# Five z1 copy buffers gated by sent stores, two attention output buffers, output weights halved earlier, and the last division taken step by step

## The chip, the cores and the metric

The kernel runs on one core of a Trainium2 chip. The metric is the device time of one execution in microseconds (us); before the change it is 1816.94 us, the median of three runs from 1816.54 to 1818.18. The core has five engines with an instruction stream each: PE (matrix products), DVE (vectors), ACT (activations and copies), POOL (vectors too) and SP, which here issues nearly all transfers. Each engine takes its instructions in the program's order, and an instruction that waits for another engine or a transfer holds up those behind it.

## The reference

The input x has 2048 rows of 576. A layer norm is followed by two branches, and their product is added to x.

```python
xn = layernorm(x)
# attention: 32 heads of 18, window of 256 keys
q, k, v = split(xn @ wqkv)
s = softmax(where(in_window, q k^T / sqrt(18), -1e9)) @ v        # then heads joined
s = s @ wo                                                       # 576 x 576
# gated unit: 2304 channels on each side
z1, z2 = split(gelu(xn @ w_in))
g = w_sp @ layernorm(z2) + b_sp                                  # 2048 x 2048 over the rows
out = x + s * silu((z1 * g) @ w_out)
```

All of it is float32, and the kernel reaches that precision by splitting operands into a high and a low part and taking several products.

## The kernel before

The program is written out engine by engine, in one long sequence. Its stages follow each other on PE: the q, k and v projections; the z2 half of the gated unit's first product (L210) up to about 430 us; the attention, 430 to 857 us; the output product with `wo` (L1314) up to about 925 us; the product over the rows (L1589) up to about 1610 us; and the last product (L1681).

**The attention stage** works in 16 units: eight groups of four heads for the first half of the rows (units 0 to 7), then the same groups for the second half (units 8 to 15). For each unit PE makes score products for the row maxima (L642), whose maxima DVE takes (L646), and the scores themselves (L787). ACT turns a bank of scores into probabilities in a `pt` tile (L791, called the exponential below), POOL blanks what is outside the window (L800, L803), and PE multiplies by the values into the accumulator `ops` (L817), in two halves of 512 columns. ACT copies each finished half into the unit's buffer `ou` (L831). Between these, PE fills in products of the z1 half of the gated unit (L723). Those end in one of seven PSUM banks (named `ma`, `mb`, `s0` to `s2`, `t0`, `t1`), which the scores use as well; DVE (L731) or ACT (L734) copies a finished block into a `z1o` buffer, of which there are three, and SP stores it (issued through L598, `z_d<-z1o` in the profile).

**The division** by the softmax sums follows each unit as a chain of nine steps: SP moves the sums out of `ou` (L867, `den<-ou`), DVE takes the reciprocal (L871), SP writes it to memory (L875, `r_d<-den`) and reads it back spread over the partitions (L879, `rp<-r_d`, four transfers; there is one `rp` buffer), POOL multiplies `ou` by it in four instructions of 256 columns (L891, the divides), and SP stores the four heads (L901, `o_d<-ou`, four transfers). There are three `ou` buffers, so the first copy of unit u waits for the stores of unit u - 3.

**What sets the order** is a planner that runs while the program is written. It keeps a `clock`, advanced by estimated PE times, and estimated finishing times of the other engines, and emits whatever is due: a score, a maximum, a group of value products, or, if nothing else is ready, one step of a z1 block (`can_fill`). SP's transfers are jobs with a due time (`issue`, `send`, `tick`); `flush` sends one at once when something is about to need it. The division steps come due `DEN_NS`, `SUM_NS` and `DIVIDE_NS` after one another, and `step(u, k)` emits at once every step of unit u up to k that has not been emitted. `step(u - 3, ...)` stands ahead of the allocation of unit u's `ou` buffer, so that the stores which that buffer waits for stand in the program before the copy. Heads of the next units are loaded by SP (L554, `att<-st_d`) and count as there `HEAD_NS` after their transfers. All these times are the planner's own; on the chip an instruction waits for its semaphores.

**Output weights and the end.** `wo` is loaded in five slices (L1097 and the ones it calls) while the last unit runs and split into two parts by DVE (L1101, L1102). The attention output is read back by `wo_load` (L1069, L1071) and split by `wo_split` (ACT L1300, DVE L1301) for the output product. The last unit's chain is emitted as far as its `rp` loads in the attention stage; its two divides stand ahead of the output product and its stores in pass 4 of 16.

Of the kernel before, what the change touches and what calls it, by code (L numbers as in the profile page):

```python
# [46 lines left out]
DIVIDE_NS = (9000, 6500, 4800)  # L47
SP_NS = 520
MOVE_NS = 5500
HEAD_NS = 5500  # L50
# [7 lines left out]
PTB = 7  # L58

# [10 lines left out]
def kernel(  # L70
# [169 lines left out]
    with ExitStack() as early:  # L240
# [283 lines left out]
        with ExitStack() as ph:  # L524
# [63 lines left out]
            sp_jobs = []  # L588
# [5 lines left out]
            def send(job, at):  # L594
                nonlocal sp_free
                sp_jobs.remove(job)
                sp_free = at + SP_NS
                job[-1]()  # L598
# [53 lines left out]
            def max_split(u):  # L652

                mx = maxima.pop(u)
                ms = halved[:, 0:64].rearrange("p (a n b) -> p a n b", a=4, n=2)
                dve.tensor_copy(ms[:, :, 0], mx)
                dve.tensor_tensor(ms[:, :, 1], mx, f32(ms[:, :, 0]), ALU.subtract)
                return use("dve", 500)
# [50 lines left out]
            def z1_rows(r):  # L709

                for f in range(FH // P):
# [7 lines left out]
                    for b in range(2):  # L719
                        bank, ps = take()  # L720
                        bank_of[r] = bank
                        for n, (w, x_) in enumerate(moving_x(wh, wl, slice(b * 512, (b + 1) * 512), r)):
# [3 lines left out]
                            if n == STEPS - 1:  # L726
                                flush(("zo", outs[0] - 3))
                                zo = zw.tile([P, 512], F32, name="z1o", bufs=3)
                                bank_of[r] = None
                                if max(busy["dve"], clock + 200) + 620 < max(busy["act"], clock + 200) + 480:  # L730
                                    dve.tensor_copy(zo, ps)  # L731
                                    bank_free[bank] = use("dve", 600, 140) + 100
                                else:
                                    act.activation(zo, ps, AF.Copy)  # L734
                                    bank_free[bank] = use("act", 480, 120) + 100
                                issue(partial(sp.dma_start, z1_tokens[f * P:(f + 1) * P, b, :, r],
                                              zo.rearrange("p (a q) -> p a q", a=2)),
                                      1000, bank_free[bank] - clock + 1300, ("zo", outs[0]))
                                outs[0] += 1
# [66 lines left out]
            def pv(u, kb, qa, qz):  # L806
# [18 lines left out]
                if kb == 4 * c + 3:  # L825
                    if c % 2 == 0:
                        step(u - 3, len(STAGES))
                        ous[u] = (ap_.tile([P, HS], F32, name="ou", bufs=3) if u < NU - 1 else
                                  tail()[:, 0:HS])
                    ou = ous[u]  # L830
                    act.activation(ou[:, c % 2 * 512:c % 2 * 512 + 512], o_ps.pop(c), AF.Copy)  # L831
                    free_at = use("act", 500, 120)
                    ops_free[0] = free_at
                    for t in later:
                        t[0] = free_at
                    if c % 2 == 1:
                        finish(u, ou)
                        if u + 2 < NU:
                            load_v(u + 2)
# [9 lines left out]
            def finish(u, ou):  # L849
# [53 lines left out]
                if u == NU - 1:  # L903
                    chain[u] = [load_den, invert, keep_den, all_sums]
                    last.extend([lambda: [divide(a, 2) for a in range(2)], lambda: [store(i) for i in range(4)]])
# [175 lines left out]
            def wow(i, k):  # L1081
                m = 5 * i + k
                return slots[2 + m // 4][:, (HS if m > 7 else 0) + m % 4 * D:(HS if m > 7 else 0) + (m % 4 + 1) * D]
# [11 lines left out]
            def load_wo(k):  # L1095
                raw = wors[k % 3]
                sp.dma_start(raw, wo[:, k, :])  # L1097

                def halve():
                    hi, lo = wow(0, k), wow(1, k)  # L1100
                    dve.tensor_copy(hi, raw)  # L1101
                    dve.tensor_tensor(lo, raw, f32(hi), ALU.subtract)  # L1102
                    use("dve", 1300)
# [7 lines left out]
            with ExitStack() as heads:  # L1111
# [74 lines left out]
                def can_fill(r):  # L1186
                    return bank_of[r] is not None or free_bank() is not None
# [31 lines left out]
                while score_queue[0] or score_queue[1] or todo or filling:  # L1219
# [43 lines left out]
                    if u == NU - 1 and n % 4 == 0 and 3 <= n // 4 < 8:  # L1263
                        wo_splits.pop(0)()
                    if u == NU - 1 and n % 4 == 0 and n // 4 < 5:
                        if n == 0:
                            step(u - 3, len(STAGES))
                            wors = [tail()[:, HS:HS + D],
                                    ap_.tile([P, HS], F32, name="ou", bufs=3)[:, :D]]
                        if n == 8:  # L1270
                            wors.append(ap_.tile([P, 10, 89], F32, name="vg").rearrange("p a b -> p (a b)")[:, :D])
                        load_wo(n // 4)
                    if u == NU - 1 and n == 28:
# [8 lines left out]
        with ExitStack() as ph:  # L1282
# [4 lines left out]
            stores = [zp.tile([P, D], F32, name="so") for _ in range(2)]  # L1287
# [30 lines left out]
            divide, store = last  # L1318
# [3 lines left out]
            divide()  # L1322
            pump(4, 5)
            for n in range(NS):
                t, c = divmod(n, 2)
                po = wo_half(0, *first_halves[0]) if n == 0 else wo_half(c * (t > 0), *halves_of[t])
                if n == 4:
                    store()
                    oraws.append(wo_load(4))
                if n in (0, 4, 6, 8):  # L1330
                    oraws.append(wo_load(3 + n // 2))
# [10 lines left out]
                so = zp.tile([P, D], F32, name="so")  # L1342
# [506 lines left out]
```

## Time and profile before

| | before |
|---|---|
| median of three runs | 1816.94 us (1816.54 to 1818.18) |
| the profiled execution: its time, and the span of its instructions | 1820.35 us, 1818.6 us |
| mean granted PE clock | 0.995 |
| PE / DVE / ACT / POOL busy | 1792.4 / 1145.2 / 930.4 / 432.0 us |

The profile comes from one execution, whose time was 3.4 us above the median; the span is the time from its first to its last instruction. A row of the waits gives engine, tile and line, what was waited for, the total in us, the number of times and the longest. A row of the chain of waits gives start, duration and what the last-ending work was doing. A row of the windows gives start and end, length, then for PE, PE's weight loads, DVE, ACT and POOL the busy time with the number of instructions, the mean granted PE clock (1.00 is full), the busy share of the transfer engines and GB/s. A row of a timeline gives start, duration, engine, line, operation, output and inputs, shapes, and in brackets how long the engine had been idle before it and what ended that.

### The profile page before, as it was taken

What the parts mean: (1) busy time and instruction counts of PE and PEld (TensorE: products, weight loads), DVE (VectorE), ACT (ScalarE), POOL (GpSimd) and SP (SyncE); (2) the same over time, 40 slices, a digit from 0 to 9 for tenths busy, and PEclk for the clock granted to TensorE, in tenths of its full rate; (3) what the DMA queues carried; (4) which work ended last, traced back from release to release, by engine and by line L of the source; (5) the groups of instructions that cost most, each with busy time, mean ns of one, the idle gap of its engine ahead of it and who ended that gap; (6) DMA issues with size and microseconds to landing.
All of it is one profiled execution on the core that took longest, in us unless ns stands there. A gap on an engine that the chain in (4) does not pass through costs nothing.

```text
span 1818.6 us, 37725 instructions
## 1 busy us (share of the span) xinstructions
PE 1792.4 (99%) x14391; PEld 1586.1 (87%) x14391; DVE 1145.2 (63%) x2322; ACT 930.4 (51%) x1737; POOL 432.0 (24%) x507
## 2 busy tenths in 40 slices
PE   9999999998999999998999999999999999999998
PEld 8989999998888888786988888888888888899998
DVE  7320243366877767663257697778876567768876
ACT  6432222224566676666467665466454534544443
POOL 3332334334456655556000000113000000000000
PEclk9999999999999999999999999999999999999999
DMA  8895779878567778756877768789786556797554
GB/s 283 201 241 155 255 257 312 271 231 265 148 188 199 206 191 198 184 151 167 257 240 239 250 216 278 263 284 300 240 271 236 174 187 208 243 275 214 155 156 137
DMA packets 266916, 405.72 MB, mean 223 GB/s; under 512 B 52336, under 2 KB 180592, under 8 KB 266608
## 3 DMA queue, kind: packets, MB, share of 16 engines
q1 hardware_dynamic: 266736, 403.32, 72.5%
q8 instruction: 113, 1.85, 0.4%
q14 instruction: 67, 0.55, 0.1%
HBM read 285.35 MB, written 117.09 MB: 221 GB/s over the span
## 4 chain that ended last, share of the span: by engine, by line
PE 85%; DMA 5%; DVE 5%; SPq 2%; issue 1%; ACT 1%; POOL 1%; DVEq 0%; ACTq 0%; POOLq 0%
PE acc L1589 31%; PE mb L210 10%; PE ma L210 10%; PE c L1681 8%; PE s L723 6%; PE ops L817 4%; PE t L723 4%; PE wops L1314 3%; PE ma L723 1%; PE s L642 1%; PE mb L723 1%; DVE spl L120 1%; DMA wr<-t_d 1%; PE s L787 1%; PE ma L384 1%
## 5 line engine op out<-in xcount | busy, mean ns | idle before, releaser
L1589 PE MATMUL acc<-spl,zh 128*128 128x512 f32 x1008 | 392.3, 389 | 0.7 <-DVE spl L120 0.7
L1589 PE MATMUL acc<-sph,zl 128*128 128x512 f32 x1008 | 392.1, 389 | 0.0
L1589 PE MATMUL acc<-sph,zh 128*128 128x512 f32 x1008 | 392.1, 389 | 0.0
L120 DVE TENSOR_TENSOR spl<-spr,sph 128x1024 fp32r<-128x1024 f32 x168 | 212.1, 1263 | 35.0 <-ACT sph L119 34.0
L1589 PEld LDWEIGHTS acc<-spl,zh 128*128 128x128 f32 x1008 | 189.2, 188 | 40.6 <-DVE spl L120 1.3
L1589 PEld LDWEIGHTS acc<-sph,zl 128*128 128x128 f32 x1008 | 189.2, 188 | 39.4
L1589 PEld LDWEIGHTS acc<-sph,zh 128*128 128x128 f32 x1008 | 189.2, 188 | 39.0
L119 ACT ACTIVATE zh<-b 128x384 fp32r<-128x384 f32 x168 | 87.6, 521 | 235.3 <-PE acc L1589 232.7
L119 ACT ACTIVATE sph<-spr 128x1024 fp32r<-128x1024 f32 x168 | 176.0, 1048 | 6.9 <-DMA spr<-sc_d 4.4
L723 PE MATMUL s<-b,z1wh 64*128 64x512 f32 x576 | 176.8, 398 | 0.0
L120 DVE TENSOR_TENSOR zl<-b,zh 128x384 fp32r<-128x384 f32 x168 | 98.6, 587 | 121.2 <-ACT zh L119 121.2
L646 DVE CUSTOM_DVE_ANT_0 s<-s,band 128x384 f32<-128x384 f32 (+2 forms) x231 | 125.2, 563 | 38.0 <-PE s L642 24.6
L1681 PE MATMUL c<-b,o 128*128 128x288 f32 x1056 | 143.1, 295 | 0.2 <-DVE o L120 0.2
L1681 PEld LDWEIGHTS c<-b,o 128*128 128x128 f32 x1056 | 140.8, 188 | 0.5 <-DVE o L120 0.4
L723 PE MATMUL t<-b,z1wh 64*128 64x512 f32 x414 | 137.0, 398 | 0.0
L791 ACT ACTIVATE pt<-s 128x384 f32<-128x384 f32 (+2 forms) x262 | 113.9, 456 | 40.6 <-PE s L787 28.6
L1046 DVE BATCH_NORM_STATS2 st<-zt 128x6 f32<-128x384 f32 x96 | 49.3, 548 | 131.8 <-ACT zt L1045 131.5
L210 PE MATMUL mb<-z2w,b 64*128 64x384 f32 x648 | 117.8, 336 | 0.0
L210 PE MATMUL ma<-z2w,b 64*128 64x384 f32 x648 | 117.7, 336 | 0.0
L800 POOL TENSOR_SCALAR_AFFINE_SELECT pt<-pt 128x512 f32<-128x512 f32 x128 | 81.8, 640 | 149.7 <-ACT pt L791 148.9
L210 PEld LDWEIGHTS mb<-z2w,b 64*128 64x128 f32 x648 | 114.1, 185 | 0.0
L210 PEld LDWEIGHTS ma<-z2w,b 64*128 64x128 f32 x648 | 114.1, 185 | 0.0
(268 smaller groups left out, 4793.5 us busy)
## 6 DMA issues: line engine op xcount, KB each, us to landing
spr<-sc_d SPq DMA_DIRECT2D x96, 512.0 KB
spr<-in_w_sp_dram SPq DMA_DIRECT2D x72, 512.0 KB
zr<-z_d SPq DMA_DIRECT2D x144, 192.0 KB
z_d<-zt SPq DMA_DIRECT2D x48, 384.0 KB
z_d<-z1o SPq DMA_DIRECT2D x72, 256.0 KB
z1t<-z_d SPq DMA_DIRECT2D x72, 256.0 KB
y_d<-z1t SPq DMA_DIRECT2D x72, 256.0 KB
a<-in_w_sp_dram SPq DMA_DIRECT2D x64, 256.0 KB
```

The lines of the kernel that those rows point to most:

```text
L119: act.activation(hi, src, AF.Copy)
L120: dve.tensor_tensor(lo, src, f32(hi), ALU.subtract)
L210: pe.matmul(banks[h][:, :n], *both[h][i], start=i == 0, stop=i == STEPS - 1)
L646: dve.tensor_tensor_reduce(out=ps[:, :w], in0=ps[:, :w], in1=band[:, m0:384], scale=1.0, scalar=-3.0e38, op0=ALU.add, op1=ALU.max, accum_o ...
L723: pe.matmul(ps, w, x_, start=n == 0, stop=n == STEPS - 1)
L791: act.activation(pt[:, j, d0:d0 + n * P], ps[:, (qa - a) * P:(qa - a + n) * P], AF.Exp, scale=scale)
L800: pool.affine_select(out=pt[:, :, 0:P], in_=pt[:, :, 0:P], pattern=[[0, 4], [1, P]], compare_op=ALU.is_ge, fill=0.0, base=0, channel_multi ...
L817: pe.matmul(o_ps[c][32 * j:32 * j + 32, (qa - 4 * c) * P:(hi - 4 * c + 1) * P], vgs[u][:, kb - k0, j * VW:j * VW + 32], pt[:, j, (qa - kb) ...
L1046: dve.bn_stats(st2[:, s, pc, :], zv)
L1314: pe.matmul(po[:, i, :288], lt[:, cs], r[:, i * 288:(i + 1) * 288], start=n == 0, stop=n == len(pl) - 1)
L1589: pe.matmul(acc[j], z[:, ps], w[:, cs], start=s == i == 0 and n in OPENS, stop=s == 7 and i == 2, skip_group_check=True)
L1681: pe.matmul(banks[key][:, :288], y, w, start=begin and k == n == 0, stop=close and k == 8 and n == 2, skip_group_check=True)
```

## The change

The constants and code change in five ways.

- `z1o` has five buffers in place of three. A z1 block may now be begun only if the store that frees its buffer has been sent, by the planner's book (`sent`). The stores come due 500 after the copy and not 1300.
- `ou` has two buffers in place of three, so unit u's first copy waits for the stores of unit u - 2, and `step(u - 2, ...)` emits their steps ahead of it.
- The planner takes loaded heads as there after 8500 and not 5500, the first unit groups' divides as due after 6500 and not 9000, and the split of the maxima as 1100 and not 500.
- The `wo` slices are loaded in unit 14 (three, into a slot that is free by then) and unit 15 (two, one of them into an `ou` buffer after the stores of unit 13), and split at five places of units 14 and 15, by DVE or ACT.
- The last unit's chain is emitted only as far as its sums. Its reciprocal, the write, the `rp` loads, the divides and the stores stand ahead of pass 0 and behind passes 0, 1, 2 and 3 of the output product; the reads of later parts move to passes 0, 5, 6, 7 and 9, and the output copies get three buffers.

The numbers of PE's instructions of each kind stay the same. Line numbers of the changed file are two or more higher: L831 becomes L833, L891 L893, L901 L903, L731 L733.

```diff
-DIVIDE_NS = (9000, 6500, 4800)
+DIVIDE_NS = (6500, 6500, 4800)
...
-HEAD_NS = 5500
+HEAD_NS = 8500
...
+ZOB = 5
...
-            sp_jobs = []
+            sp_jobs, sent = [], set()
...
             def send(job, at):
                 nonlocal sp_free
                 sp_jobs.remove(job)
+                sent.add(job[3])
...
                 dve.tensor_tensor(ms[:, :, 1], mx, f32(ms[:, :, 0]), ALU.subtract)
-                return use("dve", 500)
+                return use("dve", 1100)
...
-                                flush(("zo", outs[0] - 3))
-                                zo = zw.tile([P, 512], F32, name="z1o", bufs=3)
+                                flush(("zo", outs[0] - ZOB))
+                                zo = zw.tile([P, 512], F32, name="z1o", bufs=ZOB)
...
-                                      1000, bank_free[bank] - clock + 1300, ("zo", outs[0]))
+                                      1500, bank_free[bank] - clock + 500, ("zo", outs[0]))
...
                 if kb == 4 * c + 3:
                     if c % 2 == 0:
-                        step(u - 3, len(STAGES))
-                        ous[u] = (ap_.tile([P, HS], F32, name="ou", bufs=3) if u < NU - 1 else
+                        step(u - 2, len(STAGES))
+                        ous[u] = (ap_.tile([P, HS], F32, name="ou") if u < NU - 1 else
                                   tail()[:, 0:HS])
...
                 if u == NU - 1:
-                    chain[u] = [load_den, invert, keep_den, all_sums]
-                    last.extend([lambda: [divide(a, 2) for a in range(2)], lambda: [store(i) for i in range(4)]])
+                    chain[u] = [lambda: sp.dma_start(den, ou[DH::32, :])]
+                    last.extend([lambda: dve.reciprocal(den, den),
+                                 lambda: sp.dma_start(r_d[u].rearrange("h (a b) -> (h a) b", b=HS // 32), den),
+                                 lambda: [sums(i) for i in range(4)], lambda: [divide(a, 2) for a in range(2)],
+                                 lambda: [store(i) for i in range(4)]])
...
-            def load_wo(k):
-                raw = wors[k % 3]
-                sp.dma_start(raw, wo[:, k, :])
+            def load_wo(k, raw):
+                issue(partial(sp.dma_start, raw, wo[:, k, :]), 4000, 300, ("wo", k))
 
                 def halve():
+                    flush(("wo", k))
                     hi, lo = wow(0, k), wow(1, k)
-                    dve.tensor_copy(hi, raw)
+                    if max(busy["dve"], clock + 200) + 560 < max(busy["act"], clock + 200) + 580:
+                        dve.tensor_copy(hi, raw)
+                        use("dve", 560)
+                    else:
+                        act.activation(hi, raw, AF.Copy)
+                        use("act", 580)
                     dve.tensor_tensor(lo, raw, f32(hi), ALU.subtract)
...
                 def can_fill(r):
-                    return bank_of[r] is not None or free_bank() is not None
+                    if bank_of[r] is not None:
+                        return True
+                    n = outs[0] + 2 - bank_of.count(None) - ZOB
+                    return free_bank() is not None and (n < 0 or ("zo", n) in sent)
...
-                    if u == NU - 1 and n % 4 == 0 and 3 <= n // 4 < 8:
+                    if u == NU - 2 and n in (4, 8, 12):
+                        if n == 4:
+                            assert score_queue[1][0][0] == u
+                            wors = ab.tile([P, SLOT], F32, name="att3")
+                        load_wo(n // 4 - 1, wors[:, (n // 4 - 1) * D:n // 4 * D])
+                    if u == NU - 1 and n == 12:
+                        load_wo(3, ap_.tile([P, 10, 89], F32, name="vg").rearrange("p a b -> p (a b)")[:, :D])
+                    if u == NU - 1 and n == 20:
+                        step(u - 2, len(STAGES))
+                        load_wo(4, ap_.tile([P, HS], F32, name="ou")[:, :D])
+                    if (u, n) in ((NU - 2, 24), (NU - 2, 28), (NU - 1, 16), (NU - 1, 24), (NU - 1, 32)):
                         wo_splits.pop(0)()
...
-            divide, store = last
+            invert, keep_den, sums, divide, store = last
             zt += [z_tile(xp, k) for k in range(5)]
             units += [z_unit(zp, 0, k, s) for k in (0, 2) for s in range(8)]
             halves_of = {0: wo_split(0)}
-            divide()
+            invert()
             pump(4, 5)
             for n in range(NS):
                 t, c = divmod(n, 2)
                 po = wo_half(0, *first_halves[0]) if n == 0 else wo_half(c * (t > 0), *halves_of[t])
-                if n == 4:
+                if n in (0, 5, 6, 7, 9):
+                    oraws.append(wo_load((3, 4, 5, 6, 7)[(0, 5, 6, 7, 9).index(n)]))
+                if n == 0:
+                    keep_den()
+                if n == 1:
+                    sums()
+                if n == 2:
+                    divide()
+                if n == 3:
                     store()
-                    oraws.append(wo_load(4))
-                if n in (0, 4, 6, 8):
-                    oraws.append(wo_load(3 + n // 2))
```

Three places in the order of instructions matter below. The numbers behind the names count allocations, so that different buffers of a name can be told apart.

The first is POOL around the divides of unit 1, whose buffer is `ou_7818` before and `ou_7807` after. Before:

```order
L800 AFFINE_SELECT pt_8667<-pt_8667 128x4x128
L803 AFFINE_SELECT pt_8667<-pt_8667 128x4x128
L800 AFFINE_SELECT pt_8738<-pt_8738 128x4x128
L891 TENSOR_TENSOR ou_7818<-ou_7818,rp_8578 128x256
L800 AFFINE_SELECT pt_8773<-pt_8773 128x4x128
L891 TENSOR_TENSOR ou_7818<-ou_7818,rp_8578 128x256 x3
L800 AFFINE_SELECT pt_8805<-pt_8805 128x4x128
```

After:

```order
L802 AFFINE_SELECT pt_8555<-pt_8555 128x4x128
L805 AFFINE_SELECT pt_8555<-pt_8555 128x4x128
L802 AFFINE_SELECT pt_8581<-pt_8581 128x4x128
L805 AFFINE_SELECT pt_8581<-pt_8581 128x4x128
L893 TENSOR_TENSOR ou_7807<-ou_7807,rp_8513 128x256 x4
L802 AFFINE_SELECT pt_8607<-pt_8607 128x4x128
L805 AFFINE_SELECT pt_8607<-pt_8607 128x4x128
```

The four divides stood apart between the selects of later probabilities; now they stand in one piece, two tiles of probabilities earlier. The divides of units 2 to 5 now stand in one piece in the same way.

The second is ACT at the first `ou` copy of unit 3, which is `ou_8720` before and `ou_8697` after. Before, it waits for the stores of unit 0:

```order
L791 ACTIVATE pt_8667<-t1_8668 128x384
L831 ACTIVATE ou_8289<-ops_8387 128x512
L791 ACTIVATE pt_8667<-s2_8688 128x384
L791 ACTIVATE pt_8667<-t1_8693 128x384
L831 ACTIVATE ou_8720<-ops_8703 128x512
L791 ACTIVATE pt_8667<-t1_8733 128x384
L791 ACTIVATE pt_8738<-s0_8739 128x256
```

After, it waits for those of unit 1:

```order
L793 ACTIVATE pt_8581<-ma_8599 128x384
L793 ACTIVATE pt_8607<-t0_8608 128x384
L833 ACTIVATE ou_8255<-ops_8357 128x512
L736 ACTIVATE z1o_8630<-t1_8440 128x512
L793 ACTIVATE pt_8607<-t1_8662 128x384
L793 ACTIVATE pt_8607<-mb_8668 128x384
L833 ACTIVATE ou_8697<-ops_8672 128x512
L793 ACTIVATE pt_8607<-mb_8714 128x384
L793 ACTIVATE pt_8719<-s0_8720 128x256
```

The copy's place among the exponentials is much the same, and `ou_8697` is now the buffer of the divides shown above. From the score product that the last select ahead of those divides needs (`ma_8599`) to the last product into `ops_8672` there are 47 PE instructions; at the same place of units 4, 5, 6 and 7 there are 34, 40, 42 and 42, and in units 8 to 14 there are 78 to 121. Behind that product PE has 14 more up to the one that needs the bank of `mb_8714` again.

The third is the end of the attention, after the change. On SP, with unit 13's buffer `ou_13531` and unit 14's `ou_13991`:

```order
L869 DMA den_14037<-ou_13991 128x1x32
L881 DMA rp_14090<-r_d_67 32x1024 x4
L1074 DMA att5_14100<-o_d_66 128x4x256
L1076 DMA att5_14100<-o_d_66 64x256 x2
L600 DMA z1_d_64<-z1o_14058 128x2x256
L600 DMA z1_d_64<-z1o_14070 128x2x256
L903 DMA o_d_66<-ou_13531 18x1024 x4
L600 DMA vg_14099<-in_wo_dram 128x576
L600 DMA ou_14168<-in_wo_dram 128x576
```

and on DVE:

```order
L873 RECIPROCAL den_14037<-den_14037 128x32
L1109 CAST att3_14131<-vg_14099 128x576
L1114 TENSOR_TENSOR att3_14131<-vg_14099,att3_14131 128x576
L733 COPY z1o_14256<-s2_14062 128x512
L1109 CAST att3_14131<-ou_14168 128x576
L1114 TENSOR_TENSOR att3_14131<-ou_14168,att3_14131 128x576
L1320 TENSOR_TENSOR ohl0_14386<-att5_14100,ohl0_14386 128x4x128
```

The fourth `wo` slice (`vg_14099`) is now loaded behind the stores of unit 13, and its split on DVE stands ahead of the copy that frees bank `s2`. PE's next product into that bank is 35 instructions ahead of the output product, and the last product of unit 14 (which `den_14037` needs) is 146 ahead of it. The wait of DVE on the last unit's sums, a reciprocal that stood ahead of the first `ohl` split, now stands behind that split.

More of the change, by code (lines that the diff above doesn't have):

```diff
@@ L1081, in wow @@
             def wow(i, k):
-                m = 5 * i + k
-                return slots[2 + m // 4][:, (HS if m > 7 else 0) + m % 4 * D:(HS if m > 7 else 0) + (m % 4 + 1) * D]
+                if k == 2:
+                    return slots[4][:, HS + i * D:HS + (i + 1) * D]
+                m = 2 * (k % 3) + i
+                return slots[2 + k // 3][:, m * D:(m + 1) * D]
             def first_half(raw):
@@ L1093, in first_half @@
                 return oh, ol
-            def load_wo(k):
-                raw = wors[k % 3]
-                sp.dma_start(raw, wo[:, k, :])
+            def load_wo(k, raw):
+                issue(partial(sp.dma_start, raw, wo[:, k, :]), 4000, 300, ("wo", k))
                 def halve():
+                    flush(("wo", k))
                     hi, lo = wow(0, k), wow(1, k)
-                    dve.tensor_copy(hi, raw)
+                    if max(busy["dve"], clock + 200) + 560 < max(busy["act"], clock + 200) + 580:
[4 more added lines that the diff above has]
+                        use("act", 580)
                     dve.tensor_tensor(lo, raw, f32(hi), ALU.subtract)
-                    use("dve", 1300)
+                    use("dve", 900)
                 wo_splits.append(halve)
@@ L1262 @@
                         load_v(1)
-                    if u == NU - 1 and n % 4 == 0 and 3 <= n // 4 < 8:
-                        wo_splits.pop(0)()
[L1265 to L1273, printed above, removed]
+                    if u == NU - 2 and n in (4, 8, 12):
[9 more added lines that the diff above has]
+                    if (u, n) in ((NU - 2, 24), (NU - 2, 28), (NU - 1, 16), (NU - 1, 24), (NU - 1, 32)):
+                        wo_splits.pop(0)()
+                        if (u, n) == (NU - 1, 16):
+                            slots[3] = ab.tile([P, SLOT], F32R, name="att3")
+                    if u == NU - 1 and n == 12:
                         oraws += [wo_load(0)]
@@ L1286 @@
             zraw = [zp.tile([P, ZW], F32, name="zr", bufs=ZRB) for _ in range(ZRB)]
-            stores = [zp.tile([P, D], F32, name="so") for _ in range(2)]
+            stores = [zp.tile([P, D], F32, name="so", bufs=3) for _ in range(3)]
             ohl1 = zp.tile([P, 9, 2 * P], F32R, name="ohl1", bufs=1)
@@ L1341 @@
                     split_step(0)
-                so = zp.tile([P, D], F32, name="so")
+                so = zp.tile([P, D], F32, name="so", bufs=3)
                 act.activation(so.rearrange("p (a b) -> p a b", a=2), po[:, :, :288], AF.Copy)
```

## The prediction

> **What bounds the kernel now.** I read the busy shares first, then PE's waits, then the windows around each wait, then the chain of waits there. The page's busy line:
>
> ```profile
> PE 1792.4 (99%) x14391; PEld 1586.1 (87%) x14391; DVE 1145.2 (63%) x2322; ACT 930.4 (51%) x1737; POOL 432.0 (24%) x507
> ```
>
> PE is busy nearly always and its instructions stay the same, so the change can only add or remove time in which PE stands still, or runs at a lower clock. PE's waits:
>
> ```profile
> PE wops L1314 <- DVE ohl L1301: 5.8, 2, 5.3
> PE s L787 <- DVE z1o L731: 5.0, 1, 5.0
> PE ma L642 <- DMA att<-st_d: 3.1, 1, 3.1
> PE wops L1314 <- ACT ohl L1300: 1.9, 1, 1.9
> ```
>
> These four are all that the change can take away: 15.8 us. The windows hold the first row for the attention as a whole, then the four waits and a pause near 689 us:
>
> ```profile
> 430.00:857.00 427.00, 417.07 (x4398) 343.83 (x4395) 291.73 (x1067) 281.75 (x713) 239.65 (x351) 0.99 0.70 184
> 441.00:451.00 10.00, 9.20 (x72) 8.72 (x72) 8.86 (x34) 5.43 (x12) 2.44 (x4) 0.83 0.88 244
> 756.00:769.00 13.00, 9.90 (x69) 9.18 (x67) 7.50 (x28) 6.00 (x14) 7.94 (x12) 0.74 0.76 162
> 857.00:870.00 13.00, 7.65 (x39) 7.42 (x38) 2.83 (x5) 3.47 (x5) 2.05 (x2) 0.74 0.70 207
> 886.00:896.00 10.00, 7.61 (x55) 7.14 (x54) 1.65 (x2) 3.54 (x5) 0.00 (x0) 1.00 0.91 288
> 688.00:690.00 2.00, 1.36 (x22) 0.67 (x18) 0.81 (x4) 0.55 (x2) 2.00 (x3) 1.00 0.91 238
> ```
>
> A stall costs more than itself. Behind those of 5.0, 3.1 and 5.3 us the granted clock fell to 0.83, 0.74 and 0.74, and length times lost clock is 10 x 0.17 = 1.7, 13 x 0.26 = 3.4 and again 3.4 us. The short ones (1.9, and 0.6 of 2.0 us at 689) left it at 1.00. I take 2.5 us for each long stall, a little under the mean of 2.8, since some of it falls on time in which PE stood anyway. In the attention a PE instruction takes 427 / 4398 = 0.097 us on average; I use that to turn counts into time.
>
> **The change part by part.** *The z1 buffers.* The chain of waits at the 5.0 us stall:
>
> ```profile
> 430.96 5.45 DMA att<-st_d
> ...
> 436.47 4.49 DMA z_d<-z1o
> ...
> 441.05 0.70 DVE z1o L731
> ...
> 441.80 0.69 PE s L787
> ```
>
> A z1 copy on DVE waited for the store that frees its buffer, which stood on SP behind a head load; PE then lacked the bank. With five buffers the copy waits for a store two blocks older, and no block begins before that store is sent. Gain 5.0 + 1.7 = 6.7 us (bounds 0, if the bank is late for another reason, and 6.7). *The head loads.* At 3.1 us PE waited for heads that the planner took as there. With 3000 more it turns to other work first: 3.1 + 3.0 (its 3.4, less what fell on the stall) = 6.1 us (bounds 0 and 6.5). The larger cost of the maxima's split only shifts planned work that fills cover, as PE's busy 417.07 of 427.00 us shows: nothing, or at most one more stall of the kind at 689 (0.6).
>
> *Two `ou` buffers.* This is what decides. Before, unit 3's first `ou` copy ran on ACT as soon as its product was done, and the divides and stores of unit 1 came later:
>
> ```profile
> 533.13 0.48 ACT L791 ACTIVATE pt<-t 128x384 f32<-128x384 f32 x1
> 535.49 0.60 ACT L831 ACTIVATE ou<-ops 128x512 f32<-128x512 f32 x1 [1.88 <-PE ops L817]
> 536.04 0.49 ACT L791 ACTIVATE pt<-t 128x384 f32<-128x384 f32 x1
> ```
>
> ```profile
> 532.60 0.64 POOL L803 TENSOR_SCALAR_AFFINE_SELECT pt<-pt 128x512 f32<-128x512 f32 x1
> 539.00 0.73 POOL L891 TENSOR_TENSOR ou<-ou,rp 128x256 f32<-128x256 f32 x1
> ```
>
> ```profile
> L891 POOL TENSOR_TENSOR ou<-ou,rp x60: 722/735/749, 493.6 to 856.0; 128x256 f32<-128x256 f32 x60
> ```
>
> ```profile
> 524.87 2.43 SPq L879 DMA_DIRECT2D rp<-r_d  x4
> 528.61 2.62 SPq L679 DMA_DIRECT2D att<-mhl  x4
> 542.72 1.78 SPq L901 DMA_DIRECT2D o_d<-ou  x4
> ```
>
> ```profile
> 831.74 4.15 DMA rp<-r_d
> ...
> 859.36 2.79 DMA o_d<-ou
> 862.16 0.64 DVE ohl L1301
> ```
>
> Now the copy needs those stores landed. In the new order the four divides stand behind the select that ended at 532.60 + 0.64 = 533.24; `rp` is there by 524.87 + 2.43 + 4.15 = 531.45. So: divides 4 x 0.735 = 2.94, until 536.2; stores 1.78, until 538.0; landing 2.79, until 540.8. ACT comes to the copy at 535.5 and stands 5.3 us. The count says the same without the old times: from the score product that the select needs, an exponential (0.49), two selects (1.28), divides, stores and landing take 9.3 us; 34 to 47 PE instructions, 41 on average, give only 4.0. That is 5.3 again for each of units 3 to 7. In units 8 to 14 there are 78 or more, 7.6 us, so at most 1.7 us remain.
>
> Behind the copy (0.60) stands the exponential (0.49) of a bank that PE needs after 14 instructions (1.4 us). PE's stall is 5.3 + 0.6 + 0.5 - 1.4 = 5.0 us, with its clock 7.5; the holds of units 8 to 14 leave 1.7 + 1.1 - 1.4 = 1.4 at worst and mostly nothing. Five times: **+37.5 us**. Bounds of one stall: if the divides start as `rp` lands, at 531.45, it is 3.2; if the stores wait behind transfers such as the 2.62 us of `att<-mhl`, 7.6. With no clock loss at the one end and 3.4 at the other, 16 to 55 us for five. I take the middle, where both workings meet. A gain is excluded: a buffer fewer takes no wait away.
>
> *The end.* The views of PE and DVE at the output product's first stall, the windows row of the last 22 us, and the rows that the new order chains up:
>
> ```profile
> 854.81 2.15 PE L1314 MATMUL wops<-att,att 128*128 128x288 f32 x15
> 862.85 3.49 PE L1314 MATMUL wops<-att,ohl 128*128 128x288 f32 x13 [5.35 <-DVE ohl L1301]
> ```
>
> ```profile
> 861.90 0.35 DVE L871 RECIPROCAL den<-den 128x32 f32<-128x32 f32 x1 [10.41 <-DMA den<-att]
> ```
>
> ```profile
> 835.00:857.00 22.00, 20.91 (x211) 15.50 (x210) 11.06 (x15) 15.56 (x42) 17.72 (x23) 1.00 0.66 179
> ```
>
> ```profile
> 835.57 0.63 SPq L867 DMA_DIRECT2D den<-ou  x1
> ```
>
> ```profile
> 839.81 0.55 DVE L1101 CAST att<-vg 128x576 fp32r<-128x576 f32 x1
> 840.39 1.07 DVE L1102 TENSOR_TENSOR att<-vg,att 128x576 fp32r<-128x576 f32 x1
> ...
> 846.57 0.69 DVE L731 COPY z1o<-t 128x512 f32<-128x512 f32 x1 [1.29 <-PE t L723]
> ```
>
> The split for the product stood on DVE behind the last unit's reciprocal, which waited 10.41 us for its sums. Behind the split it no longer holds PE: 5.8 + 3.4 = 9.2 us go, and with earlier reads the 1.9. But a new chain ends on DVE. At 20.91 / 211 = 0.099 us, unit 14's last product is 146 x 0.099 = 14.5 us ahead of the output product's 854.8, at 840.3. Then copy 0.6, `den` 0.6, `rp` loads 2.4 and landing 4.15, divides 2.9, stores 1.8, the fourth `wo` slice 0.4 and about 2.8 to land (an estimate, as for the store), split 0.55 + 1.07, z1 copy 0.7: 858.3. PE wants that bank 35 x 0.099 = 3.5 us ahead of 854.8, at 851.3. A stall of 7.0; I take 6, as part of the issue time overlaps, and 2.5 of clock: 8.5 against 11.1 gone, **-2.6 us** (bounds -11.1, if `wo` lands in time, and +1.3, if PE stalls 9 us and loses 3.4 of clock). The steps put behind passes 0 to 3 sit in a stage where POOL is all but idle (2.05 of 13 us); nothing.
>
> **Sum**: 1818.6 - 6.7 - 6.1 + 37.5 - 2.6 = 1840.7 us of span. The execution's time was 1.75 above its span and 3.4 above the median, so 1840.7 + 1.75 - 3.4 = **1839 us** against 1816.94.
>
> [...]
>
> **The rivals.** Two groups of the attention (430 to 860 us) bear on them and on what follows, with busy time, mean ns and the idle time ahead by what ended it:
>
> ```profile
> L831 ACT ACTIVATE ou<-ops 128x512 f32<-128x512 f32 x30 | 18.1, 605 | 31.2 <-PE ops L817 25.8 <-issue 2.2 <-DMA r_d<-den 1.7
> ```
>
> ```profile
> L800 POOL TENSOR_SCALAR_AFFINE_SELECT pt<-pt 128x512 f32<-128x512 f32 x128 | 81.8, 640 | 149.7 <-ACT pt L791 148.9 <-DMA att<-st_d 0.8
> ```
>
> *First, the other side: ACT never stands long at the copy.* If PE or ACT reach it 5 us later than in the old trace, only the gains remain: 1839 - 37.5 = 1801.5 us. For it: units 8 to 14 have the room, and a PE stall appears only where the hold passes 1.4 - 1.1 = 0.3 us. Against it: the counts of 34 to 47, and POOL, by the groups of the attention's window, waits for ACT's exponentials (148.9 us), so its divides cannot run far ahead of ACT. It decides below 15.4 / 5 = 3.1 us of loss per unit. *Second, the stalls come but the clock mostly stays:* 1839 - 5 x 2.5 = 1826.5. For it: 441 to 451 lost only 1.7, and the stalls would be near the size at which the clock falls. Against: three of three stalls of 3.1 us and over. *Third, the stores come later still,* behind `att<-mhl`, or one of the old stalls stays: 1839 + 5 x 2.6 = 1852, or 1839 + 6.7 = 1846. For it: SP takes its transfers in order, and the `mhl` loads wait for DVE. Against: SP was not held up there in the old trace.
>
> **How the numbers follow.** The forecast 0.58, the first rival 0.20, the second 0.14, the third 0.08. The forecast's own range is 1825 to 1853. For 8 in 10 I go from 1803, which takes in half of the first rival, to 1855, the upper bound of the five stalls. What can be told from no change is 0.2%, 3.6 us. Faster comes from the first rival, 0.20; within 0.2% is the lower bound of the five stalls, 16 against 15.4 gained, 0.04 taken from the second; slower is the rest, 0.76.
>
> **What would show it.** In the profile after, PE's waits should have about five rows' worth of stalls of 4 to 6 us at the score product L789, ended by ACT's exponentials (L793), one in each of units 3 to 7; ACT's copies L833 should have idle time ended by the stores `o_d<-ou` (some 26 us, where L831 had 1.7 by a transfer), and the granted clock should dip behind each. The waits on DVE `z1o`, on `att<-st_d` and on `ohl` should be gone, and one on `z1o` should stand just ahead of the output product. If L833 waits only for PE, the forecast is wrong and the first rival holds; if the clock stays at 1.00 behind the stalls, the second.

## The result and the profile after

The changed kernel takes 1841.91 us, the median of four runs (1839.68 to 1846.57), against 1816.74 for the kernel before on the same chip: a ratio of 1.0142, with a 95% interval of 1.012 to 1.0165. It is slower by some 25 us. The profiled execution has a span of 1839.2 us, 20.6 more than before, and a mean PE clock of 0.988.

The waits of PE after the change (columns as before):

```profile
PE s L789 <- ACT pt L793: 11.2, 4, 3.7
PE mb L789 <- ACT pt L793: 9.4, 2, 5.7
PE s L789 <- DVE z1o L733: 4.1, 1, 4.1
PE wops L1333 <- ACT ohl L1319: 1.8, 1, 1.8
...
PE s L789 <- ACT z1o L736: 1.6, 1, 1.6
```

and the longest wait of ACT there:

```profile
ACT ou L833 <- DMA o_d<-ou: 33.9, 6, 8.2
```

ACT stands 33.9 us, in six waits, at the copies into `ou` for the stores that free the buffer. PE stands 20.6 us, five times long and once briefly, for exponentials (`ACT pt`) that are queued behind those copies. The wait on head loads is gone, the waits on DVE's `ohl` split, behind the reciprocal, are down from 5.8 to 0.4 us, and the z1 wait of 5.0 us is down to 1.6. A new one of 4.1 us stands on a z1 copy just ahead of the output product. PE's busy time, 1792.4 us before, is 1801.6 with the same instructions: of the 20.6 us, 9.2 are slower running and 11.4 more standing.

One of the five places, unit 3's first copy, by the timelines of ACT, POOL, SP and PE, and by the chain of waits:

```profile
526.08 0.49 ACT L793 ACTIVATE pt<-mb 128x384 f32<-128x384 f32 x1
532.43 0.60 ACT L833 ACTIVATE ou<-ops 128x512 f32<-128x512 f32 x1 [5.87 <-DMA o_d<-ou]
```

```profile
525.98 2.83 POOL L893 TENSOR_TENSOR ou<-ou,rp 128x256 f32<-128x256 f32 x4
```

```profile
528.84 1.36 SPq L903 DMA_DIRECT2D o_d<-ou  x4
```

```profile
529.88 2.45 DMA o_d<-ou
```

```profile
526.04 2.15 PE L819 MATMUL ops<-pt,vg 128*32 128x384 f32 x32
...
533.46 0.58 PE L789 MATMUL mb<-att 56*128 56x256 f32 x1 [3.67 <-ACT pt L793]
```

The four divides run without a gap behind the select, the stores go out behind them, 2.45 us after the last was issued they have landed, and ACT's copy starts at 532.43. PE had finished the product that the copy reads at 526.04 + 2.15 = 528.2, ran its 14 further instructions, and then stood 3.67 us until the exponential behind the copy was done.

The windows around the five stalls, and those of the attention and the output product, after the change:

```profile
528.00:545.00 17.00, 13.33 (x134) 11.12 (x128) 9.35 (x36) 6.26 (x17) 3.31 (x6) 0.90 0.54 154
558.00:574.00 16.00, 12.40 (x118) 10.16 (x118) 8.69 (x32) 5.85 (x16) 3.14 (x5) 0.89 0.42 108
587.00:603.00 16.00, 12.39 (x113) 10.11 (x106) 7.55 (x26) 4.70 (x13) 3.56 (x6) 0.79 0.34 86
618.00:637.00 19.00, 13.31 (x114) 10.99 (x112) 8.18 (x28) 5.62 (x15) 5.17 (x8) 0.73 0.39 104
652.00:668.00 16.00, 12.29 (x106) 10.21 (x105) 7.85 (x28) 5.98 (x18) 3.72 (x6) 0.79 0.44 113
668.00:860.00 192.00, 191.59 (x2065) 156.65 (x2064) 128.97 (x464) 134.71 (x355) 114.23 (x167) 1.00 0.71 180
866.00:880.00 14.00, 9.22 (x92) 5.56 (x89) 3.93 (x7) 6.29 (x19) 6.74 (x12) 0.76 0.62 174
421.20:879.50 458.30, 431.21 (x4444) 355.16 (x4440) 295.96 (x1079) 284.65 (x717) 241.87 (x352) 0.96 0.69 177
879.50:943.30 63.80, 61.59 (x454) 61.02 (x450) 16.02 (x21) 31.98 (x45) 4.13 (x5) 0.97 0.78 250
```

and the last two stages in the kernel before:

```profile
421.10:853.00 431.90, 421.97 (x4443) 347.81 (x4439) 295.35 (x1077) 286.31 (x721) 241.43 (x351) 0.99 0.70 186
853.00:923.40 70.40, 62.66 (x452) 61.96 (x449) 16.02 (x21) 31.42 (x45) 5.36 (x6) 0.95 0.74 238
```

The attention takes 26.4 us longer and the output product 6.6 less; the rest of the program differs by less than 1. All of the loss lies in the five windows and in the last 14 us of the attention: from 668 to 860 us, units 8 to 13, PE is busy 191.59 of 192.00 us at full clock.

The low clock comes in periods. Windows cut to them, with the 3.4 us ahead of the fourth:

```profile
533.10:536.50 3.40, 3.04 (x17) 3.04 (x19) 1.43 (x5) 1.74 (x5) 1.23 (x2) 0.51 0.95 270
563.90:567.30 3.40, 3.40 (x22) 3.40 (x21) 2.24 (x7) 1.48 (x5) 1.32 (x3) 0.50 0.34 88
591.20:598.00 6.80, 5.43 (x29) 5.34 (x31) 2.99 (x10) 3.06 (x9) 1.86 (x3) 0.50 0.15 43
618.50:621.90 3.40, 1.43 (x13) 1.00 (x10) 2.17 (x8) 0.00 (x0) 2.17 (x4) 1.00 0.57 156
621.90:632.10 10.20, 6.48 (x34) 6.39 (x36) 3.56 (x11) 4.15 (x11) 1.86 (x3) 0.50 0.12 32
656.00:662.80 6.80, 5.84 (x31) 5.84 (x33) 3.12 (x10) 3.79 (x10) 1.86 (x3) 0.50 0.33 79
871.10:877.90 6.80, 4.30 (x43) 2.23 (x47) 3.80 (x7) 1.83 (x5) 0.64 (x1) 0.50 0.59 169
```

In the six low rows the clock is 0.50 or 0.51, for 3.4, 6.8 or 10.2 us. What PE loses by that is half of the time in which it is busy there, an estimate from these rows: 12.1 of 24.2 us behind the five stalls, and 2.1 of 4.3 us behind the one at the end. The time in which it stands there is not counted.

### The profile page after: what moved, and what is told of

It is laid out like the page before. It is cut to its first block, busy times and chain, and to the rows that moved or that the text cites. A ratio compares the mean times of both kernels' runs of the same rounds, so it can differ in the third digit from the quotient of the medians.

```text
span 1839.2 us, 37691 instructions
## 1 busy us (share of the span) xinstructions
PE 1801.6 (98%) x14391; PEld 1593.7 (87%) x14391; DVE 1146.3 (62%) x2326; ACT 929.5 (51%) x1733; POOL 432.3 (24%) x507
## 3 DMA queue, kind: packets, MB, share of 16 engines
q8 instruction: 113, 1.85, 0.4%
## 4 chain that ended last, share of the span: by engine, by line
PE 82%; DMA 9%; DVE 3%; ACT 2%; POOL 2%; SPq 1%; issue 1%; ACTq 0%; POOLq 0%; DVEq 0%
PE acc L1613 34%; PE ma L211 17%; PE c L1705 8%; PE s L725 5%; PE mb L211 3%; PE ops L819 3%; DMA att<-st_d 2%; PE ma L725 2%; PE wops L1333 2%; PE t L725 1%; DMA wr<-t_d 1%; PE mb L725 1%; DMA rp<-r_d 1%; POOL ou L893 1%; DMA o_d<-ou 1%
## 5 line engine op out<-in xcount | busy, mean ns | idle before, releaser
L725 PE MATMUL s<-b,z1wh 64*128 64x512 f32 x666 | 198.5, 399 | 0.0
L648 DVE CUSTOM_DVE_ANT_0 s<-s,band 128x384 f32<-128x384 f32 (+2 forms) x204 | 109.7, 555 | 53.5 <-PE s L644 29.1
L793 ACT ACTIVATE pt<-s 128x384 f32<-128x384 f32 (+2 forms) x240 | 103.9, 451 | 41.6 <-PE s L789 22.7
L648 DVE CUSTOM_DVE_ANT_0 t<-t,band 128x384 f32<-128x384 f32 (+2 forms) x174 | 96.9, 569 | 41.2 <-PE t L644 23.2
L725 PE MATMUL s<-b,z1wl 64*128 64x512 f32 x333 | 120.7, 398 | 0.0
L725 PEld LDWEIGHTS s<-b,z1wh 64*128 64x128 f32 x666 | 112.7, 189 | 3.9 <-issue 1.4
```

The costliest lines, as they stand in the source:

```text
L648: dve.tensor_tensor_reduce(out=ps[:, :w], in0=ps[:, :w], in1=band[:, m0:384], scale=1.0, scalar=-3.0e38, op0=ALU.add, op1=ALU.max, accum_o ...
L725: pe.matmul(ps, w, x_, start=n == 0, stop=n == STEPS - 1)
L793: act.activation(pt[:, j, d0:d0 + n * P], ps[:, (qa - a) * P:(qa - a + n) * P], AF.Exp, scale=scale)
```

## The experiments

Each time is compared with runs of the kernel before on the same chip, whose medians were 1819.08 (first four), 1818.23 (next four) and 1819.38 us (last two). Ratios to it are given with their 95% intervals.

**Three `ou` buffers again.** This one gives up the two new `z1o` buffers for the third `ou` buffer.

```diff
-ZOB = 5
+ZOB = 3
...
-                        step(u - 2, len(STAGES))
-                        ous[u] = (ap_.tile([P, HS], F32, name="ou") if u < NU - 1 else
+                        step(u - 3, len(STAGES))
+                        ous[u] = (ap_.tile([P, HS], F32, name="ou", bufs=3) if u < NU - 1 else
...
```

> The change with three ou buffers again (step u - 3) and, since both do not fit, three z1o buffers, still gated. Theory (the two ou buffers are the cost): ACT's copies wait for no store, the five stalls of 3.6 to 5.7 us and their clock loss (35.7 us in the profile after) go; the fourth wo slice is no longer behind unit 13's stores, so the stall ahead of the output product (4.1 + 3.4) goes too: 1841.9 - 35.7 - 7.5 = 1799 us, or about 1805 if three z1o buffers bring the old 5.0 us stall back. Rival (the other constants and the new order make the stalls): it stays at 1835 to 1842 us.

It took 1824.98 us, 1.0037 (1.0025 to 1.0048). Neither of the two. No `ou` copy waits for `o_d<-ou` any more (one waits 1.5 us, which the profile puts down to a z1 store) and the five stalls are gone, but the rest of the gain did not come. The waits of PE and of ACT, ACT's timeline at the one long stall, and windows of the places with a low clock:

```profile
PE t L644 <- ACT pt L793: 4.7, 1, 4.7
```

```profile
ACT z1wh L748 <- DMA z1raw<-in_w_z_dram: 7.6, 2, 5.1
```

```profile
565.18 0.52 ACT L748 ACTIVATE z1wh<-z1raw 128x384 fp32r<-128x384 f32 x1 [5.06 <-DMA z1raw<-in_w_z_dram]
```

```profile
441.00:446.00 5.00, 5.00 (x37) 4.97 (x35) 3.33 (x13) 2.85 (x7) 1.72 (x3) 0.66 0.71 183
845.00:850.00 5.00, 5.00 (x24) 2.94 (x27) 0.35 (x1) 5.00 (x14) 3.39 (x6) 0.74 0.85 242
850.00:855.00 5.00, 5.00 (x36) 2.06 (x28) 2.44 (x4) 2.29 (x7) 2.14 (x4) 0.57 0.34 119
```

The stall of 4.7 us is of the same make as the five: an instruction on ACT waits for a transfer (here a z1 weight), and the exponentials stand behind it. And the z1 products, the filling, ran out early: their last instruction starts at 838.38 us, 24.5 us ahead of the output product (12 us after the change, 7 before it). What is left then are scores whose exponentials keep ACT busy for 5.00 of 5.00 us (845 to 850) while PE has 24 instructions, at a clock of 0.74 and then 0.57.

**Two `ou` buffers in the kernel before, and nothing else.**

```diff
-                        step(u - 3, len(STAGES))
-                        ous[u] = (ap_.tile([P, HS], F32, name="ou", bufs=3) if u < NU - 1 else
+                        step(u - 2, len(STAGES))
+                        ous[u] = (ap_.tile([P, HS], F32, name="ou") if u < NU - 1 else
...
```

> The kernel before with two ou buffers (step u - 2) and nothing else. Theory: 30 to 47 PE instructions stand between the score that the last select ahead of the divides needs and the product ahead of the copy, in units 3 to 7, so ACT waits 5 to 6 us five times, PE stalls 3.6 to 5.7 us and loses about 3 us of clock each time: 5 x 7.1 = 36, 1817 + 36 = 1853 us. Rival (it needs the other parts of the change): within 5 us of 1817.

It took 1868.11 us, 1.0275 (1.0255 to 1.0294): the theory's direction and more than its size. ACT's wait, with L831 in this file's numbers, and one of PE's:

```profile
ACT ou L831 <- DMA o_d<-ou: 50.8, 8, 9.5
```

```profile
PE ops L817 <- ACT ou L831: 9.6, 2, 8.7
```

Eight copies waited, not five, one of them in the last units, where PE stood 8.7 us. The edit alone is enough for a loss of 49 us, and together with the other parts of the change it is about half of that.

**Heads taken as there after 8500, in the kernel before.** The edit is `HEAD_NS = 8500`.

> The kernel before with loaded heads taken as there after 8500 and not 5500, nothing else. Theory: the wait on att<-st_d (3.1 us and 3.4 of clock) goes and nothing else moves: 1817 - 6 = 1811 us. Rival (the new order makes another wait for it): 1815 us or more with a wait of another name in the attention.

It took 1815.83 us, 0.9985 (0.9973 to 0.9997): 3 us less, not 6. The wait on head loads went, and so did the 5.3 us one at the output product; 5.7 us on `DVE z1o`, a new 2.9 us on ACT's last copy and a new 1.4 us on DVE's maxima stand in the profile. By its words the rival came true, 1815 us or more with waits of other names.

**Three `ou`, five `z1o` and six `pt` buffers.** On top of the first experiment:

```diff
-PTB = 7
+PTB = 6
-ZOB = 3
+ZOB = 5
```

> The change with three ou buffers and five z1o buffers, paid for with six pt tiles in place of seven. Theory: no wait on ou; with the z1o waits gone as well 1797 to 1801 us, if six pt tiles are enough. Rival (the pt tiles become the bound): ACT's exponentials wait for the value products, and it takes 1810 us or more.

It took 1816.12 us, 0.9978 (0.9962 to 0.9994). The time is the rival's, but not for its reason. The attention is down to 426.0 us, the clock there is 1.00, and nothing waits on `pt` tiles. But the output product takes 68.7, with 4.6 us of waits on ACT's split:

```profile
421.20:847.20 426.00, 421.70 (x4443) 341.89 (x4440) 294.04 (x1076) 286.92 (x720) 242.40 (x350) 1.00 0.74 190
847.20:915.90 68.70, 62.71 (x450) 61.39 (x450) 17.04 (x21) 31.76 (x46) 6.51 (x6) 0.98 0.72 234
```

It differs from the change in the third `ou` buffer and one `pt` tile fewer, and its ratio is 0.9978 where the change has 1.0142: some 30 us. What the tile alone does is tested below.

**Only the gate on z1 blocks, in the kernel before.**

```diff
...
-                    return bank_of[r] is not None or free_bank() is not None
+                    if bank_of[r] is not None:
+                        return True
+                    n = outs[0] + 2 - bank_of.count(None) - 3
+                    return free_bank() is not None and (n < 0 or ("zo", n) in sent)
...
-                                      1000, bank_free[bank] - clock + 1300, ("zo", outs[0]))
+                                      1500, bank_free[bank] - clock + 500, ("zo", outs[0]))
```

> The kernel before, with three z1o buffers, and only the rule that a z1 block begins once the store that frees its buffer was sent, with the stores due 500 after the copy (slack 1500). Theory (the gate, not the number of buffers, removes the z1o stall): the 5.0 us stall falls to 1.6 to 1.9 us as in the change and in the run with three gated buffers, without its 1.7 us of clock: about 5 us less than before. Rival (the two further buffers did it): the stall of 5.0 stays, and the time is within 2 us of before.

It took 1832.1 us, 1.0082 (1.0063 to 1.01). Both were wrong. The z1o stall did fall, to 2.2 us, but the order that the gate gives has new waits, and the largest of ACT's waits for a transfer in the attention is again on a weight, 14.7 us in six waits:

```profile
ACT z1wh L747 <- DMA z1raw<-in_w_z_dram: 14.7, 6, 8.1
```

```profile
PE s L788 <- ACT pt L792: 7.8, 3, 4.3
...
PE ma L788 <- ACT z1o L735: 2.2, 1, 2.2
```

Of the 10.0 us between this profile and that of the kernel before, PE stands 4.4 and is busy 5.6 longer; what made its busy time longer was not traced.

**Six `pt` tiles in the kernel before.** The edit is `PTB = 6`.

> The kernel before with six pt tiles in place of seven, nothing else. Theory (what the run with three ou, five z1o buffers and six pt tiles gained against before comes from the z1o, head and end parts): within 3 us of before, with the 5.0, 3.1 and 5.3 us stalls still there. Rival (six pt tiles give another order, and that is the gain): 4 us or more below before, with one of those stalls gone.

It took 1817.28 us, 0.9989 (0.9973 to 1.0005): no difference in time, as the theory had it, though against its account the profile lost the 3.1 and the 5.3 us stalls. Its profiled span of 1812.2 us lies well under its median, so no more is read from it. The six tiles do not explain what the next run gained.

**Three `ou`, five `z1o`, six `pt` buffers, and `HEAD_NS = 7000`.**

> The change with three ou buffers, five z1o buffers, six pt tiles, and loaded heads taken as there after 7000 in place of 8500. Theory: the attention keeps the 426 us that it took with 8500, since no stall there was a wait on heads, and other work stands at the output product, whose waits on ohl (6.0 us with 8500) decide: between 0.993 and 0.998 of before. Rival (7000 is too early for the heads): the wait on att<-st_d of 3.1 us comes back, and it is at 1.000 of before or over.

It took 1804.32 us, 0.9935 (0.9918 to 0.9951), within the theory's range, the fastest of all and faster than both kernels. The attention takes 422.6 and the output product 61.0 us, both with a clock of 1.00:

```profile
421.40:844.00 422.60, 419.84 (x4443) 340.86 (x4441) 292.02 (x1081) 285.52 (x716) 244.76 (x356) 1.00 0.74 193
844.00:905.00 61.00, 59.90 (x447) 59.44 (x448) 15.96 (x21) 31.67 (x45) 2.54 (x2) 1.00 0.79 252
```

**The fourth `wo` slice ahead of unit 13's stores.**

```diff
                     if u == NU - 1 and n == 12:
                         load_wo(3, ap_.tile([P, 10, 89], F32, name="vg").rearrange("p a b -> p (a b)")[:, :D])
+                        flush(("wo", 3))
```

> The change as it is, but the transfer of the fourth wo slice is put into SP's order at once, so that it stands ahead of unit 13's stores. Theory (that slice waits for those stores, its split holds the z1 copy on DVE, and PE lacks the bank): DVE's wait of 11.4 us for vg, PE's stall of 4.1 us ahead of the output product and the 3.4 us of clock behind it go: 1.010 of before in place of 1.014, the five stalls at the ou copies unchanged. Rival (something else is late there): a stall of about 4 us stays at that place.

It took 1843.26 us, 1.0152 (1.0128 to 1.0175), no less than the change. The named stall did go: DVE's wait for that slice fell from 11.41 us to 3.20, as the two rows show (first after the change, then in this run), and PE no longer waits on DVE's z1 copy.

```profile
870.97 0.46 DVE L1109 CAST att<-vg 128x576 fp32r<-128x576 f32 x1 [11.41 <-DMA vg<-in_wo_dram]
863.02 0.46 DVE L1109 CAST att<-vg 128x576 fp32r<-128x576 f32 x1 [3.20 <-DMA vg<-in_wo_dram]
```

```profile
421.00:876.50 455.50, 429.48 (x4442) 352.68 (x4440) 295.52 (x1079) 284.52 (x717) 242.03 (x351) 0.97 0.69 176
876.50:943.90 67.40, 62.74 (x452) 61.35 (x449) 15.60 (x21) 31.22 (x45) 5.43 (x6) 0.97 0.77 252
```

The attention got 2.8 us shorter and the output product 3.6 longer. Its passes wait for the `ohl` splits, and PE, which came to them earlier, waited there instead: 3.0 us on ACT's, where it had been 1.8, and 1.6 on DVE's, where it had been 0.4.

So the `wo` slice explains the stall at that place, and not the time of the end.

**Half of the divides on DVE, in units 1 to 5.**

```diff
-                    pool.tensor_tensor(ou[:, hs], ou[:, hs], rp()[:, hs], ALU.mult)
+                    (dve if 1 <= u <= 5 and a >= 2 else pool).tensor_tensor(ou[:, hs], ou[:, hs], rp()[:, hs], ALU.mult)
```

> The change as it is, but in units 1 to 5 the last two of the four divides run on DVE beside POOL's two, at the same place. Theory (the copy waits for divides, stores and landing in a row): POOL's part falls from 2.94 to 1.47 us, so ACT's holds at L833 fall by about 1.5 us each (33.9 to about 27 in all) and PE's five stalls from 3.6 to 5.7 us to 2.1 to 4.2; four of five then end below 3 us and should lose no clock, so that 5 x 1.5 + 4 x 2.5 = 17 us go: 1.005 of before. Without the clock part 7 us go: 1.010. Rival (the hold hangs on something else than the divides, such as the SP queue): the holds stay at 5.6 us on average, 1.014 of before.

It took 1842.86 us, 1.0132 (1.0112 to 1.0151), which cannot be told from the change. The divides got shorter by less than expected: a divide took DVE 952 ns at the median, where the shortest took 411. POOL's own were longer beside DVE's, as in unit 4's division (second row).

```profile
L893 DVE TENSOR_TENSOR ou<-ou,rp x10: 411/952/1000, 526.8 to 649.2; 128x256 f32<-128x256 f32 x10
L893 POOL TENSOR_TENSOR ou<-ou,rp x2: 918/943/968, 616.9 to 617.8; 128x256 f32<-128x256 f32 x2
```

At unit 1's division POOL began at 526.12 and DVE ended at 526.83 + 1.33 = 528.16, about 2.0 us where POOL alone had taken 2.83. But the stores landed 3.08 us after the last was issued, not 2.45, and ACT's copy started at 532.45, where it had been 532.43.

```profile
529.27 3.08 DMA o_d<-ou
```

```profile
ACT ou L833 <- DMA o_d<-ou: 36.4, 8, 7.8
```

ACT's wait for the stores did not fall to 27 us: it is 36.4 in eight copies, and the five long holds come to 31.5 us, where they were 32.8. PE's five stalls were 3.5, 3.4, 2.6, 4.3 and 4.0 us, and the window around the one of 2.6 us shows low clock, 0.89, as well:

```profile
588.00:604.00 16.00, 13.44 (x128) 10.83 (x122) 9.14 (x36) 6.47 (x17) 2.49 (x4) 0.89 0.43 111
```

That stalls below 3 us lose no clock was an estimate, and this row is against it. The theory missed: as the rival had it, the holds stayed nearly as they were, and the experiment moved the cost too little to judge by the time.

**The first `ou` copy on DVE, in units 3 to 7.**

```diff
-                    act.activation(ou[:, c % 2 * 512:c % 2 * 512 + 512], o_ps.pop(c), AF.Copy)
+                    if c % 2 == 0 and 3 <= u <= 7:
+                        dve.tensor_copy(ou[:, 0:512], o_ps.pop(c))
+                    else:
+                        act.activation(ou[:, c % 2 * 512:c % 2 * 512 + 512], o_ps.pop(c), AF.Copy)
```

> The change as it is, but the first ou copy of units 3 to 7 runs on DVE and no longer on ACT. Theory (what costs is the queue behind a waiting instruction): the wait for the stores moves to DVE, ACT's wait on o_d<-ou falls from 33.9 us to a few, and PE stalls about as long as before, 13 instructions later at a score product for the maxima whose bank DVE frees behind the copy: five stalls of 3 to 6 us released by DVE's maxima (L648), 1.012 to 1.017 of before. Rival (ACT is what cannot be held, DVE has the slack): the stalls fall under 1.5 us and it is at 0.995 to 1.003 of before.

It took 1844.94 us, 1.0156 (1.0133 to 1.018), as the theory had it. ACT's wait moved to DVE, and PE waits for maxima in place of exponentials, five times from 3.8 to 6.5 us:

```profile
DVE ou L834 <- DMA o_d<-ou: 33.7, 5, 7.9
```

```profile
PE t L644 <- DVE mx L648: 16.2, 3, 6.5
PE ma L644 <- DVE mx L648: 5.0, 1, 5.0
PE s L644 <- DVE mx L648: 4.2, 1, 4.2
```

What costs is the queue behind the waiting copy, on whichever of the two engines it stands.

## Why the prediction was right

The forecast was 1839 us, slower than before; the measured time is 1841.91 us. By its steps:

- **What bounds.** Right. All of the difference, 11.4 us of standing and 9.2 of slower running, lies in stalls and in the clock behind them.
- **The five holds at the copies.** Right in mechanism and in the units, too large in size. ACT stood 5.87 us at unit 3's copy against 5.3 forecast, but it had been idle for 1.6 us of that before the product ended. PE's stalls came out shorter, 20.3 us for the five (3.67, 3.60, 3.61, 5.69 and 3.71) against 25. The mis-sized term is the stores with their landing: 1.78 + 2.79, together 4.6 us, taken from two rows of the kernel before. After the change the copy starts 3.6 us after the first store's issue (528.84 to 532.43), and 3.45 to 3.89 us at the other four places. The clock came out as forecast: length times lost clock in the five windows is 1.7, 1.8, 3.4, 5.1 and 3.4, together 15.4 us, but in part of it PE stood anyway, and 12.1 are left against 12.5. Sum 32.4 against 37.5.
- **The z1 buffers.** 5.0 us with 1.7 of clock became 1.6 without: 5.1 gained of 6.7. The runs do not say that the gate and the buffers are worth this by themselves: the gate alone, with three buffers, lost 0.8%.
- **The head loads.** The stall and its 3.4 us went, 6.5 against 6.1. As an edit by itself it gained 3 us.
- **The end.** Here the term was wrong by some 3 us: -2.6 forecast. The new stall came where the chain had put it, at 868.8 us, ahead of the output product, with 4.1 us in place of 6, another of 0.7, and 2.1 of clock: 6.9 us, against 8.5 forecast. The step that failed is the other side of it: I let all of 11.1 us go, but the output product got only 6.6 us shorter: 1.8 us on ACT's split, 0.4 on DVE's and some clock remain. That makes +0.3.
- **The sum.** 32.4 - 5.1 - 6.5 + 0.3 = 21.1 us, where the profiles differ by 20.6 and the forecast had 22.1. That the sum came so near is in part luck: the holds were taken 5.1 us too dear and the gain of the z1 buffers 1.6 too large, but the end was taken 2.9 too cheap and the head loads 0.4 too small. The medians differ by 25 us and not 20.6, mostly because the profiled execution of the kernel before was 3.4 us above its median.

The first rival fell with ACT's 33.9 us. The second, no loss of clock, fell with the windows. All five gaps, from 3.6 to 5.7 us, lost clock, and the period at 621.9 us came although PE had been busy for 1.43 of the 3.4 us ahead of it. No run shows a length of stall from which on the clock falls: in the first experiment it fell behind stalls of 1.85 and 1.75 us, and before the change it stayed at 1.00 behind one of 1.9 us. The third rival shows once, in part: ahead of the divides of unit 4, for which unit 6's copy waits, POOL stood 2.51 us for a transfer (which one the profile only infers), and that stall is the longest, 5.69 us.

```profile
617.86 2.81 POOL L893 TENSOR_TENSOR ou<-ou,rp 128x256 f32<-128x256 f32 x4 [2.51 <-DMA z_d<-z1o]
```

What stays open is what sets the time of the end. Taking away its stall gave nothing back, and what the stepwise last division is worth was not measured alone. Nor were the five `z1o` buffers, the earlier divides (`DIVIDE_NS`) and the larger cost of the maxima's split run by themselves.

## What to carry to other kernels

A buffer less makes its next writer wait for the whole chain that empties it; count the instructions that the critical engine has between the chain's start and that writer, turn them into time, and compare it with the chain's length (here 4 us against 9). The price is then paid by what is queued behind the waiting instruction, here on ACT and on DVE alike, and by the clock after the stall (here 12.1 us, by the estimate above). An edit that only alters a planner's rules or constants gives a new order with waits of its own, so its parts do not add up, and each order has to be run.

## What the runs showed of the hardware that I had not expected

The clock fell behind shorter stalls than those of the kernel before. In the first experiment stalls of 1.85 and 1.75 us were followed by low clock (0.66 over the 5 us from 441 us, 0.77 over the 6 us from 476), while the stalls of 1.9 us before the change and of 1.6 us after it, at 449 us, were not:

```profile
443.00:456.00 13.00, 11.38 (x120) 9.18 (x118) 9.61 (x38) 7.41 (x19) 5.90 (x9) 1.00 0.93 228
```

And there it fell with no stall that the profile shows, to 0.57 from 850 to 855 us, where PE had only scores and value products left. A busy share of 5.00 of 5.00 us in the profile does not exclude that.

The losses behind the five stalls, 1.7, 1.8, 3.4, 5.1 and 3.4 us, lie near multiples of 1.7 us. The windows cut to the periods show why: in this execution the clock is 0.50 or 0.51 for 3.4, 6.8 or 10.2 us, once, twice or three times 3.4. The starts of the six, 533.1, 563.9, 591.2, 621.9, 656.0 and 871.1 us, lie whole multiples of 3.41 us apart, as far as windows of a tenth of a us can tell. Short windows show the edges of the longest:

```profile
621.70:621.90 0.20, 0.00 (x0) 0.00 (x0) 0.00 (x0) 0.00 (x0) 0.00 (x0) 0.96 0.72 164
621.90:622.10 0.20, 0.00 (x0) 0.00 (x0) 0.00 (x0) 0.00 (x0) 0.00 (x0) 0.50 0.17 61
632.00:632.20 0.20, 0.20 (x5) 0.15 (x2) 0.20 (x2) 0.00 (x1) 0.00 (x0) 0.69 0.90 302
632.10:635.50 3.40, 3.40 (x50) 1.86 (x48) 1.54 (x7) 0.77 (x2) 0.64 (x1) 1.00 0.83 202
```

Divides of 128 x 256 took longer where DVE and POOL ran them side by side. On DVE one took 952 ns at the median of ten and 411 at the shortest; at unit 1's division, where DVE's two took 1.33 us together, the last 0.62 us of them lie behind the end of POOL's two at 526.12 + 1.42 = 527.54. POOL's two of unit 4 took up to 968 ns beside DVE's, where POOL's median over all fifty is 736.
